# Unit 0's first two steps by chunks, seven products from unit 4, sums planned apart and a new order of work

## The chip, the cores and the metric

The kernel runs on one core of a Trainium2 chip. The metric is the device time of one execution in microseconds (us); of several runs the median is taken. An engine of the core runs its own queue of instructions in the order in which the program issued them, and waits on semaphores for the others: TensorE (PE, with its weight loads shown apart as PEld), VectorE (DVE), ScalarE (ACT), GpSimd (POOL) and SyncE (SP), which issues the transfers.

## The reference

A gated linear attention is followed by a layer pair. With B=4, H=8, S=768, D=48 and everything in fp32:

```python
for t in range(S):
    state = alpha[:, :, t, :, None] * state + np.einsum('bhd,bhe->bhde', k[:, :, t], v[:, :, t])
    y[:, :, t] = np.einsum('bhd,bhde->bhe', q[:, :, t], state)
# x: y as 3072 tokens x 384
h = x @ w_in               # 384 x 2048
g = h - np.tanh(h)
out = g @ w_out            # 2048 x 384
```

The two weight matrices arrive as float64 and are converted on the chip; the kernel computes in fp32.

## The kernel before, in words

The 3072 tokens are cut into 12 units of 256 tokens (three to a batch), and a unit into two chunks of 128. "u.c" names a chunk of a unit, "u:s" a step of a unit.

*Attention of a unit.* alpha, k and q (aT, kT, qT) are brought to columns by head and time. In units 0 and 1 TensorE does it with products by the identity ("turn aT", "turn kT", "turn qT", line 749) and a copy follows (line 753); later units load 32-row pieces, which ACT widens ("wide") and DVE transposes ("flip", line 717). DVE then runs scans over alpha: U (suffix products, line 796), "ends" (lines 804 and 805) and W (prefix products, line 815); k is multiplied by U ("kU") and q by W ("qW", line 761; in unit 0 each in halves a and b). "size" (line 824, ACT) squares U and W for a check of their range, "least" (DVE) does the same for the ends. TensorE makes "back" (k turned back for the update), copied out by ACT ("natural"), "scores" (line 884 in unit 0), which DVE masks ("masked", lines 908 and 911), "carried" (the product with the decayed state), the "update" of the state (line 1088), and "y". ACT copies y out as x ("x"), and DVE the part of it that is missing ("rest", line 1046 from unit 2 on); "moves" on SP brings rows together. From unit 2 on scores of a chunk and y of the chunk before are one visit of TensorE.

*The layers of a unit.* Eight steps of 256 hidden columns. "first" is the first product (line 1285 where plain: 12 matmuls of 128x256 per step); then ACT runs three passes over a 128x512 tile, "bend" (tanh, line 1326), "turn" (arctan, line 1329) and "square" (line 1334), and DVE multiplies by h ("shrunk", line 1338): that is g to the accuracy asked. "large" (line 1343, ACT, every second step) checks the range. "second" adds g @ w_out into four banks of PSUM, o0 to o3.

*Fewer products.* In units 0 and 1 "second" is plain (line 1361, four matmuls of 128x384 per step; unit 0 in o0 and o1, unit 1 in o2 and o3). From unit 2 on it is done with seven 128x192 products in place of eight (line 1383), for which DVE forms differences of g ("sums", lines 1350 and 1351) and, once, sums of w_out ("combine"). From unit SEVEN on (line 462, 3 before) "first" is done in such a way too: "first_a" (line 1298, four 128x128 products), a copy of one of them by ACT ("keep", line 1303), three dependent sums on DVE in one task ("partial", lines 1307 to 1309), "first" (lines 1314 and 1316) and a last sum on DVE ("join", line 1321). "weigh" prepares w_in for it once, "mix" x once per unit.

*The weights.* Sixteen pieces, in0 to in7 and out0 to out7, are fetched by SP into a pool of four buffers (line 45) and converted by two passes on ACT ("read_a", "read", lines 89 and 92) and two on DVE ("bits", line 96, and one that is named by the piece, such as "in0", line 99). A later part of the kernel loads them again to check their range ("reload", "look").

*The order.* Each of these is a task with an engine, a cost in microseconds, a rank and tasks that it follows. The order in which all tasks are issued is written out by hand as a list of steps (STEPS, line 335). Only inside the first stage does the planner add something: where its own sum of costs leaves TensorE idle before "y 0.0", it puts in small products of no use ("spin", line 1479, in bank o2). A tile of a pool with a fixed number of buffers (two banks "h" for first products, one pair "sc" for scores and y, o0 to o3) makes its next user wait for the last reader of the one before.

At the start the loads are issued as aT 0, v 0, kT 0, qT 0, in0, aT 1, in1, in2, in3, kT 1, qT 1, out0 and so on. Unit 0's steps use whole 256-token tiles, but for "first 0:0", which is made by chunks ("first_a 0:0" after "x 0.0", "first 0:0" after "x 0.1").

## Time and profile before

| | us |
|---|---|
| median of 3 runs (558.57 to 559.6) | 558.87 |
| profiled execution, whole | 563.36 |
| its span, first to last instruction | 561.6 |

| stretch of the profiled span (us) | length | PE busy | DVE busy | ACT busy | PE clock |
|---|---|---|---|---|---|
| 0 to 6.78 | 6.78 | 5.20 | 3.39 | 1.90 | 1.00 |
| 23.84 to 43.90 | 20.06 | 18.02 | 15.62 | 16.38 | 1.00 |
| 270.00 to 540.00 | 270.00 | 270.00 | 241.65 | 177.36 | 1.00 |

The stretches between these are in the prediction. In a row of groups of the profile stand the line of the kernel, the engine, the operation, "out<-in" by the program's tile names, the shape and the number of instructions; then busy time and mean length, and at the end the idle time of the engine before them with what released it. A wait written "PE h L1314 <- DVE w L1321: 1.7, 1, 1.7" says that TensorE, before the product of line 1314, waited 1.7 us in all, once, 1.7 at the longest, for DVE's instruction of line 1321. "issue" stands for idle time for which the profile shows no wait. A row of windows gives the stretch, its length, then busy time (and instructions) of PE, PEld, DVE, ACT and POOL, the granted clock of TensorE, the share of time in which the transfer engines were busy, and GB/s. In a timeline a row is the start, the time, engine, line and operation, and in brackets the idle time before it.

### The profile page before, as it was taken

The numbers are of one execution on the slowest core, as the hardware profiler recorded it, in microseconds if no ns is written. First come the engines' busy times: TensorE is split into PE (matmuls) and PEld (weight loads), VectorE is DVE, ScalarE is ACT, GpSimd is POOL, SyncE is SP. The second block draws the span as 40 slices with busy tenths as digits, with TensorE's granted clock in tenths as the row PEclk, the third lists the DMA queues.
The fourth block names the chain that finished last, engine by engine and source line by source line (L and its number), as shares of the span: only waits on it lengthen the run. The fifth ranks groups of instructions, "written<-read, shape, count | busy, mean of one in ns | idle before, by whom it ended". The sixth has DMA issues, their size and how long they took to land. (4 is left out here: it accounts for less than half of the span.)

```text
span 561.6 us, 15127 instructions
## 1 busy us (share of the span) xinstructions
PE 547.5 (97%) x6191; PEld 501.3 (89%) x6191; DVE 484.8 (86%) x1032; ACT 393.2 (70%) x746; POOL 4.9 (1%) x23
## 2 busy tenths in 40 slices
PE   7989999999999999998999999999999999999995
PEld 6877777777999999998999999999999999999995
DVE  7578659999989899999899999999999976796773
ACT  2589898967868768978668876757955654566460
POOL 3000000000000000000000000000000000000000
PEclk9699999999999999999999999999999999999999
DMA  9988482225264473535164251123020000100001
GB/s 219 240 202 245 169 204 84 88 65 146 52 135 101 114 128 107 115 117 140 35 121 113 85 157 50 48 48 85 15 51 1 30 2 8 36 2 1 30 2 33
DMA packets 60236, 50.90 MB, mean 91 GB/s; under 512 B 35552, under 2 KB 49920, under 8 KB 60160
## 3 DMA queue, kind: packets, MB, share of 16 engines
q1 hardware_dynamic: 57536, 49.07, 34.3%
q8 instruction: 51, 0.84, 0.6%
q10 hardware_dynamic: 2624, 0.79, 0.6%
q14 instruction: 25, 0.20, 0.1%
HBM read 44.04 MB, written 4.72 MB: 87 GB/s over the span
## 5 line engine op out<-in xcount | busy, mean ns | idle before, releaser
L1383 PE MATMUL o<-b,e 128*128 128x192 f32 x480 | 94.0, 326 | 0.0
L1326 ACT ACTIVATE z<-w 128x512 f32<-128x512 f32 x72 | 45.1, 626 | 54.8 <-DVE w L1321 54.7
L1383 PEld LDWEIGHTS o<-b,e 128*128 128x128 f32 x480 | 80.1, 190 | 0.8
L1383 PE MATMUL o<-w_out,e 128*128 128x192 f32 x320 | 78.6, 327 | 0.0
L1316 PE MATMUL h<-xT,w_in 128*128 128x256 f32 x288 | 74.1, 380 | 0.0
L1383 PE MATMUL o<-b,g 128*128 128x192 f32 x320 | 69.9, 326 | 0.0
L1285 PE MATMUL h<-xT,w_in 128*128 128x256 f32 (+1 forms) x300 | 66.2, 374 | 2.0 <-DVE g L1338 1.7
L1285 PEld LDWEIGHTS h<-xT,w_in 128*128 128x128 f32 x300 | 54.4, 190 | 10.9 <-DVE g L1338 1.8
L1329 ACT ACTIVATE z<-z 128x512 f32<-128x512 f32 x96 | 60.5, 630 | 1.8
L1334 ACT ACTIVATE u<-z 128x512 f32<-128x512 f32 x96 | 60.4, 629 | 1.9
L1321 DVE TENSOR_TENSOR w<-h,u 128x512 f32<-128x512 f32 x72 | 49.0, 681 | 11.8 <-PE h L1316 11.1
L1383 PEld LDWEIGHTS o<-w_out,e 128*128 128x128 f32 x320 | 55.7, 190 | 1.5
L1298 PE MATMUL h<-xT,w_in 128*128 128x128 f32 x288 | 56.4, 278 | 0.6 <-DVE w L1321 0.5
L1298 PE MATMUL h<-xT,w_out 128*128 128x128 f32 x288 | 55.8, 275 | 0.3 <-DVE xT L1245 0.3
L1383 PEld LDWEIGHTS o<-b,g 128*128 128x128 f32 x320 | 54.1, 190 | 0.4
L1316 PEld LDWEIGHTS h<-xT,w_in 128*128 128x128 f32 x288 | 49.2, 191 | 3.7
L1338 DVE TENSOR_TENSOR g<-w,u 128x512 f32<-128x512 f32 x72 | 48.8, 680 | 3.9 <-ACT u L1334 3.6
L1343 ACT ACTIVATE big<-u 128x1024 f32<-128x1024 f32 x48 | 50.7, 1055 | 0.9
L1298 PEld LDWEIGHTS h<-xT,w_in 128*128 128x128 f32 x288 | 46.7, 191 | 2.4 <-DVE w L1321 0.8
L1350 DVE TENSOR_TENSOR e<-g 128x384 f32<-128x384 f32 x80 | 43.8, 548 | 3.8 <-PE o L1383 3.3
L1303 ACT COPY u<-h 128x128 f32<-128x128 f32 x72 | 18.8, 262 | 38.2 <-PE h L1298 32.2
L1298 PEld LDWEIGHTS h<-xT,w_out 128*128 128x128 f32 x288 | 43.7, 192 | 0.5 <-DVE xT L1245 0.5
(177 smaller groups left out, 1134.9 us busy)
## 6 DMA issues: line engine op xcount, KB each, us to landing
raw<-in_moe_w_out_dram SPq DMA_DIRECT2D x16, 768.0 KB, 4.9
raw<-in_moe_w_in_dram SPq DMA_DIRECT2D x48, 96.0 KB, 4.4
raw<-in_moe_w_in_dram SPq DMA_DIRECT2D x16, 288.0 KB, 5.2
vt<-in_v_dram SPq DMA_DIRECT2D x23, 192.0 KB, 3.9
ar<-in_alpha_dram SPq DMA_DIRECT2D x20, 192.0 KB, 3.2
kr<-in_k_dram SPq DMA_DIRECT2D x20, 192.0 KB, 3.3
qr<-in_q_dram SPq DMA_DIRECT2D x20, 192.0 KB, 3.0
raw<-in_moe_w_in_dram SPq DMA_DIRECT2D x16, 192.0 KB, 4.3
```

What stands on the lines that cost most here:

```text
L1285: T.matmul(h[:, a, to], lhsT=w_in[:, j, f * P:(f + 1) * P], rhs=xT[u][:, j, to], start=(j == 0), stop=(j == KT - 1))
L1298: T.matmul(h[:, i], lhsT=left[n][:, s], rhs=right[u][n], start=i == 0, stop=True, skip_group_check=True)
L1303: A.copy(m["kept", s][:, 0], m["part", s][:, 0])
L1316: T.matmul(h[:, 2 * a:2 * a + 2].rearrange("p i t -> p (i t)"), lhsT=wi[:, KT - 1, s, a], rhs=xT[u][:, KT - 1, :], start=False, stop=True, ...
L1321: V.tensor_add(m["w", s], m["h", s].rearrange("p i t -> p (i t)"), m["u", s])
L1326: A.activation(m["z", s], m["h", s], AF.Tanh, scale=TA / W_SCALE)
L1329: A.activation(m["z", s], m["z", s], AF.Arctan, scale=TB)
L1334: A.activation(m["u", s], m["z", s], AF.Square, scale=TK * W_SCALE ** -0.5)
L1338: V.tensor_mul(g.rearrange("p a c t -> p (a c t)"), m["h", s], m["u", s])
L1343: A.activation(big, m["us", s // 2].rearrange("p s t -> p (s t)"), AF.Relu, bias=-F_FAST, scale=W_SCALE, accum_out=over[:, n:n + 1])
L1350: V.tensor_sub(e[:, 0:3, :], x[:, 3:4].to_broadcast([P, 3, P]), x[:, 0:3])
L1383: T.matmul(o[n][:, i], lhsT=g_, rhs=w_, start=(s_ == 0 and (n, i) in ((0, 0), (1, 0), (2, 1), (3, 0))), stop=(s_ == FS - 1), skip_group_ch ...
```

## The change

The attention of units 0 and 1 and the first steps are arranged anew, and the plain and the seven-product form change places in one unit:

- SEVEN goes from 3 to 4: unit 3's first products are plain, unit 3 has no "mix", "keep", "partial" and "join", and "weigh" moves one unit later.
- "rest" from unit 4 on is a copy on ACT, no longer on DVE.
- The three dependent sums of "partial" become three tasks, partial_a, partial_b and partial, which the order can place apart.
- Steps 0:0 and 0:1 (PARTED = 2) are made by chunks all the way: first, bend, turn, square, shrunk and second each stand once per chunk, with tiles of half the size ("first_a", "bend_a", ..., "second_0").
- Unit 0's output is in banks o2 and o1 and unit 1's in o0 and o3. The turns of unit 1, its "back" and its y use banks 0 and 3 in place of 2 and 3; "turn kT 1" follows "x 0.1" in place of "y 0.1".
- v 0 is loaded after kT 0 and qT 0, in0 after aT 1. The loads are now issued as qT 0, aT 0, kT 0, qT 1, aT 1, v 0, in0, in1, in2, kT 1, in3, v 1, out0 and so on.
- The planner's costs of some tasks are other numbers, and STEPS is a new list. On TensorE it opens with five spins, turn qT 0, turn aT 0, turn kT 0, five spins, back 0.0, a spin, update 0.0, scores 0.0, back 0.1, turn aT 1, scores 0.1, y 0.0, carried 0.1, update 0.1, y 0.1, turn qT 1, first_a 0:0, first 0:0, first_a 0:1, turn kT 1, first 0:1, back 1, first 0:2, first 0:3, scores 1.0, second_0 0:0, second 0:0, y 1.0.

```diff
...
     STEPS = (
...
     )
...
     PLAIN = 2
-    SEVEN = 3
+    PARTED = 2
+    SEVEN = 4
     BOTH_QUEUES = 0
...
-            add(f"fetch {what}{s}", "SP", 2.5 if both else 4.0 if what == "in" else 2.3, rank - 30, [held and f"read {held[0]}{held[1]}", held and f"bits {held[0]}{held[1]}"],
+            add(f"fetch {what}{s}", "SP", 2.5 if both else 4.0 if what == "in" else 2.3, rank - 30, [held and f"read {held[0]}{held[1]}", held and f"bits {held[0]}{held[1]}", n == 0 and "load aT 1"],
                 lambda what=what, s=s, both=both: fetch(what, s, False if both else None), lat=2.4)
...
             there = [f"fetch {what}{s}", both and f"upper {what}{s}", older and f"{older[0]}{older[1]}"]
-            add(f"read_a {what}{s}", "ACT", 1.05, rank, there, lambda do=do: do(0))
...
+            add(f"read_a {what}{s}", "ACT", 0.96, rank, there, lambda do=do: do(0))
...
 
...
                    [what < 3 and u > 0 and not by_matmul(u - 1, what) and not by_matmul(u, what) and f"{name}{prev}"]
-                   + [u == 1 and ("kUb 0" if what == 3 else "turn qT 0")]
+                   + [u == 1 and ("kUb 0" if what == 3 else "turn qT 0")] + [u == 0 and what == 3 and x for x in ("load kT 0", "load qT 0")]
                    + [f"{last} {u - 2}.{CU - 1}" if last != "y" or u - 2 < PLAIN else y_of((u - 2, CU - 1)) for last in ("y", "state") if what == 3 and u > 1
...
                     else:
-                        t = ps_o.tile([P, NP, P], FP32, name="turned", tag=f"o{2 * u + c}")
+                        t = ps_o.tile([P, NP, P], FP32, name="turned", tag=f"o{(0, 3)[c]}" if u else f"o{c}")
                     m["turned", what, c] = t.rearrange("p g (n i) -> p g i n", n=CU)
...
             if by_matmul(u, 1):
-                go("turn kT", "PE", 1.0, 1, ["load kT"] + [later and x for x in ("x 0.0", "y 0.1", "state 0.1")], lambda: turn(1))
+                go("turn kT", "PE", 1.0, 1, ["load kT"] + [later and x for x in ("x 0.0", "x 0.1", "state 0.1")], lambda: turn(1))
             if by_matmul(u, 2):
...
 
-                    m["y", c] = banks((2, 3))
+                    m["y", c] = banks((0, 3))
                     y = [m["y", c][b].rearrange("p g t -> p (g t)") for b in range(2)]
...
                         to = bass.AP(t.tensor, t.offset, [t.ap[0], (2 * TU + HP, 2), (1, HP)])
-                        V.tensor_copy(to, m["y", c].rearrange("p r g t -> p r (g t)")[0:ROWS, :, NP * (HP + D):])
+                        (A.copy if u >= 4 else V.tensor_copy)(to, m["y", c].rearrange("p r g t -> p r (g t)")[0:ROWS, :, NP * (HP + D):])
                         return
...
                     go_c("x", "ACT", 0.66, 10, [y, f"first {u - 2}:{FS - 1}"], features)
-                    go_c("rest", "DVE", 0.26, 10.5, [y, f"first {u - 2}:{FS - 1}"], rest)
+                    go_c("rest", "ACT" if u >= 4 else "DVE", 0.27, 10.5, [y, f"first {u - 2}:{FS - 1}"], rest)
                     return
...
             def back():
-                m["tp"] = banks((2, 3))
+                m["tp"] = banks((0, 3))
                 for c in range(CU):
...
 
+                parted = u == 0 and s < PARTED
+
+                def of_chunk(x, c):
+                    return x.rearrange("p (a t) -> p a t", a=2)[:, :, c * P:(c + 1) * P]
+
                 def first(to=slice(None)):
...
                                      start=(j == 0), stop=(j == KT - 1))
+                    m["h3", s] = h
                     m["h", s] = h if to.stop == P else h.rearrange("p a t -> p (a t)")
...
 
-                def partial():
+                def partial(n):
                     kept, part = m["kept", s], m["part", s]
-                    V.tensor_add(kept[:, 1], kept[:, 0], part[:, 1])
-                    V.tensor_add(kept[:, 2], kept[:, 1], part[:, 2])
-                    V.tensor_add(kept[:, 1::2], kept[:, 1:3], part[:, 3:4].to_broadcast([P, 2, P]))
+                    if n < 2:
+                        V.tensor_add(kept[:, n + 1], kept[:, n], part[:, n + 1])
+                    else:
+                        V.tensor_add(kept[:, 1::2], kept[:, 1:3], part[:, 3:4].to_broadcast([P, 2, P]))
 
...
 
-                def bend():
-                    m["z", s] = two.tile([P, 2 * TU], FP32, name="z")
-                    A.activation(m["z", s], m["h", s], AF.Tanh, scale=TA / W_SCALE)
+                def bend(c=None):
+                    if not c:
+                        m["z", s] = two.tile([P, 2 * TU], FP32, name="z")
+                    z, h = m["z", s], m["h", s]
+                    if c is not None:
+                        z, h = of_chunk(z, c), m["h3", s][:, :, c * P:(c + 1) * P]
+                    A.activation(z, h, AF.Tanh, scale=TA / W_SCALE)
+
+                def turn(c=None):
+                    z = m["z", s] if c is None else of_chunk(m["z", s], c)
+                    A.activation(z, z, AF.Arctan, scale=TB)
 
-                def turn():
-                    A.activation(m["z", s], m["z", s], AF.Arctan, scale=TB)
-
-                def square():
-                    if not seven:
+                def square(c=None):
+                    if not seven and not c:
                         take_u()
-                    A.activation(m["u", s], m["z", s], AF.Square, scale=TK * W_SCALE ** -0.5)
-
-                def shrunk():
-                    g = m["g", s] = three.tile([P, 2, CU, P], FP32, name="g")
+                    u_, z = m["u", s], m["z", s]
+                    if c is not None:
+                        u_, z = of_chunk(u_, c), of_chunk(z, c)
+                    A.activation(u_, z, AF.Square, scale=TK * W_SCALE ** -0.5)
+
+                def shrunk(c=None):
+                    if not c:
+                        m["g", s] = three.tile([P, 2, CU, P], FP32, name="g")
+                    g = m["g", s]
+                    if c is not None:
+                        h = m["h3", s][:, :, c * P:(c + 1) * P]
+                        V.tensor_mul(g[:, :, c, :], h, of_chunk(m["u", s], c))
+                        return
                     V.tensor_mul(g.rearrange("p a c t -> p (a c t)"), m["h", s], m["u", s])
...
                     if plain:
-                        if s == 0:
-                            m["o"] = [ps_o.tile([P, d_model], FP32, name=f"o{CU * u + c}") for c in range(CU)]
+                        if s == 0 and not of.start:
+                            m["o"] = [ps_o.tile([P, d_model], FP32, name=f"o{((2, 1), (0, 3))[u][c]}") for c in range(CU)]
                         for a in range(2):
                             f = 2 * s + a
-                            for c in range(CU):
+                            for c in range(CU)[of]:
                                 T.matmul(m["o"][c], lhsT=g[:, a, c, :],
...
                     plan.takes[f"first_a {me}"] = f"partial {me}"
-                plan.takes[f"first_a {me}" if u == s == 0 else f"first {me}"] = f"join {me}" if seven else f"shrunk {me}"
+                plan.takes[f"first_a {me}" if parted else f"first {me}"] = f"join {me}" if seven else f"shrunk {me}"
                 bank = None if older[2] else f"masked 0.{CU - 1}"
...
                     add(f"first_a {me}", "PE", 0.87, r, [bank, f"mix {u}", "weigh 1", late], seven_a)
-                    add(f"keep {me}", "ACT", 0.26, r + 0.1, [f"first_a {me}"] + old_u, keep)
-                    add(f"partial {me}", "DVE", 0.75, r + 0.2, [f"keep {me}"], partial)
+                    add(f"keep {me}", "ACT", 0.2, r + 0.1, [f"first_a {me}"] + old_u, keep)
+                    add(f"partial_a {me}", "DVE", 0.2, r + 0.2, [f"keep {me}"], lambda: partial(0))
+                    add(f"partial_b {me}", "DVE", 0.2, r + 0.21, [f"partial_a {me}"], lambda: partial(1))
+                    add(f"partial {me}", "DVE", 0.34, r + 0.22, [f"partial_b {me}"], lambda: partial(2))
                     add(f"first {me}", "PE", 1.51, r + 0.3, [f"first_a {me}", "weigh 2"], seven_b)
-                    add(f"join {me}", "DVE", 0.65, r + 0.7, [f"first {me}", f"partial {me}", older[2] and f"shrunk {older[2]}"], join)
-                elif u == s == 0:
+                    add(f"join {me}", "DVE", 0.61, r + 0.7, [f"first {me}", f"partial {me}", older[2] and f"shrunk {older[2]}"], join)
+                elif parted:
                     add(f"first_a {me}", "PE", 1.35, r, [f"in{s}", bank, "x 0.0"], lambda: first(slice(0, P)))
...
 
-                add(f"bend {me}", "ACT", 0.55, r + 0.9, [f"join {me}" if seven else f"first {me}", older[2] and f"square {older[2]}"], bend)
-                add(f"turn {me}", "ACT", 0.54, r + 0.92, [f"bend {me}"], turn)
-                add(f"square {me}", "ACT", 0.54, r + 0.95, [f"turn {me}"] + ([] if seven else old_u), square)
-                add(f"shrunk {me}", "DVE", 0.61, r + 1, [f"square {me}", older[3] and f"second {older[3]}"], shrunk)
+                if parted:
+                    for c, x in enumerate(("_a", "")):
+                        before = [f"{{}}_a {me}"] * c
+                        add(f"bend{x} {me}", "ACT", 0.32, r + 0.9, [f"first{x} {me}"] + [b.format("bend") for b in before], lambda c=c: bend(c))
+                        add(f"turn{x} {me}", "ACT", 0.32, r + 0.92, [f"bend{x} {me}"], lambda c=c: turn(c))
+                        add(f"square{x} {me}", "ACT", 0.32, r + 0.95, [f"turn{x} {me}"] + [b.format("square") for b in before], lambda c=c: square(c))
+                        add(f"shrunk{x} {me}", "DVE", 0.34, r + 1, [f"square{x} {me}"] + [b.format("shrunk") for b in before], lambda c=c: shrunk(c))
+                else:
+                    add(f"bend {me}", "ACT", 0.55, r + 0.9, [f"join {me}" if seven else f"first {me}", older[2] and f"square {older[2]}"], bend)
+                    add(f"turn {me}", "ACT", 0.54, r + 0.92, [f"bend {me}"], turn)
+                    add(f"square {me}", "ACT", 0.54, r + 0.95, [f"turn {me}"] + ([] if seven else old_u), square)
+                    add(f"shrunk {me}", "DVE", 0.61, r + 1, [f"square {me}", older[3] and f"second {older[3]}"], shrunk)
                 if s % 2:
...
                          + ([f"second {u}:{s - 1}"] if s else []))
+                if parted:
+                    older_a = [f"second_0 {u}:{s - 1}"] if s else []
+                    add(f"second_0 {me}", "PE", 1.29, r + 5, [f"out{s}", f"shrunk_a {me}"] + older_a, lambda: second(slice(0, 1)))
+                    add(f"second {me}", "PE", 1.29, r + 5.1, [f"shrunk {me}", f"second_0 {me}"] + needs, lambda: second(slice(1, 2)))
+                    return
                 parts = [7] if not seven or (u == NU - 1 and s >= FS - 2) else [2, 4, 5, 7]
```

## The prediction

> **What bounds the kernel now.** I read the page's totals and slices first, then the waits of TensorE alone, then windows cut where those waits lie, then the order of time on single engines.
>
> ```profile
> PE 547.5 (97%) x6191; PEld 501.3 (89%) x6191; DVE 484.8 (86%) x1032; ACT 393.2 (70%) x746; POOL 4.9 (1%) x23
> ...
> PEclk9699999999999999999999999999999999999999
> ```
> ```profile
> PE y L1088 <- issue: 1.9, 1, 1.9
> PE h L1314 <- DVE w L1321: 1.7, 1, 1.7
> PE h L1285 <- DVE g L1338: 1.7, 1, 1.7
> ```
> ```profile
> 6.78:13.60 6.82, 5.07 (x149) 4.07 (x147) 6.75 (x13) 2.03 (x5) 0.00 (x0) 1.00 1.13 248
> 13.60:23.84 10.24, 10.07 (x107) 8.38 (x111) 5.24 (x10) 4.92 (x10) 0.00 (x0) 0.50 0.91 216
> ...
> 27.20:43.90 16.70, 14.65 (x214) 12.89 (x213) 13.13 (x24) 14.23 (x23) 0.00 (x0) 1.00 0.84 211
> 43.90:204.00 160.10, 160.10 (x1758) 132.75 (x1757) 139.04 (x258) 131.46 (x233) 0.00 (x0) 1.00 0.50 127
> 204.00:270.00 66.00, 63.39 (x735) 59.99 (x735) 62.78 (x140) 53.59 (x108) 0.00 (x0) 1.00 0.46 116
> ```
> TensorE (PE) is the bound: from 43.9 to 204 it never rests. So time leaves only if the first 43.9 us shrink, if the rests at 204 to 270 (66.00 - 63.39 = 2.6) go, or if TensorE gets less work. VectorE (DVE) runs at 62.8 of 66 in that stretch: it causes those rests. In the opening TensorE rests for 1.92 us at 11.6 inside "update 0.0" for no wait that the profile shows, and from 13.60 to 23.84 its clock is 0.50.
>
> **The change, part by part.** The sum is made against the profiled execution (span 561.6, whole run 563.36) and then carried to the median of the plain runs, 558.87, which lies 4.5 us lower. Where those 4.5 us lie the profile can't say. If they are the rest at 11.6 and its half clock, what their removal brings is not there to be won from the median.
>
> *Seven products from unit 4, not 3.* Eight steps of unit 3 become plain.
>
> ```profile
> 82.26 5.34 PE L1285 MATMUL h<-xT,w_in 128*128 128x256 f32 x24
> 87.44 1.78 PE L1361 MATMUL o<-w_out,g 128*128 128x384 f32 x5
> ```
> Two plain steps take 87.44 - 82.26 = 5.18, one 2.59. A seven-product step is 0.89 ("first_a", 189.60 to 190.49) and 1.53 ("first", 200.58 to 202.11): 2.42. Eight steps cost TensorE 8 x 0.17 = +1.3 us, and all of it is on the path. DVE loses eight joins of 0.60, eight partial sums of 0.97 and one mix of 1.05 (start to start): 13.6 us.
>
> *"rest" to ScalarE (ACT) from unit 4.* 16 copies of 0.28 (line 1046, 279 ns): DVE 4.5 us less, ACT 4.5 more, in an engine at 53.6 of 66. It stands on ACT beside "x", which waited 11.3 us in all for TensorE, so I price it at nothing on the path; if each held up the next visit it would cost 4.5. DVE is rid of 18 us in all, mostly between 160 and 480. That should end the rests at 204 to 270: from -2.6 to +2 (a new order may put another wait there, and the largest there now is 1.7). I take -2.2.
>
> *The partial sums planned apart* add no instruction: three sums as before, now free to stand between other work. Priced inside the last item.
>
> *Opening.* q is loaded first, alpha second, v sixth. Now alpha's turn starts at 4.08 and takes 2.27; the copy starts at 6.43. In the new order the turn of q stands there, alpha's follows at 6.27 (partly at the faster rate of k's turn, 1.16) and the copy starts at 7.82: the scans begin 1.4 us later. The order of DVE from there:
>
> ```profile
> 6.43 0.69 DVE L753 COPY aT<-turned 128x512 f32<-128x512 f32 x1 [1.66 <-PE turned L749]
> 7.06 2.35 DVE L796 TENSOR_TENSOR_SCAN U<-aT,after 128x516 f32<-128x516 f32 x2
> 9.34 0.13 DVE L804 TENSOR_TENSOR ends<-U,low 128x4 f32<-128x4 f32 x1
> ...
> 16.69 1.29 DVE L908 TENSOR_TENSOR pm<-scores,mask 128x512 f32<-128x512 f32 x2 [2.10 <-PE scores L884]
> ...
> 20.17 1.29 DVE L908 TENSOR_TENSOR pm<-scores,mask 128x512 f32<-128x512 f32 x2 [1.46 <-PE scores L884]
> ```
> With start-to-start times: copy 0.63, two scans 2.30, both ends 0.54, kUa 0.58, Wa 1.16, kUb 0.58, qWa 0.58, Wb 1.15, least 0.1, qWb 0.6, decay 0.3: the first mask could start at 16.35 where it now waits until 16.69 for scores that run at half clock. If the clock stays whole, the scores are ready and DVE goes on: mask 1.25, bits 0.5, unit 1's copy 0.63 and a wait of 0.3 for its turn (whose bank qWb frees at 16.7), second mask 1.25: ends at 20.3 against 21.46. From there to the last kUb of unit 1: two scans 2.3, two bits 1.0, in0 to in2 2.75, ends, least, state and decay 1.1, two W scans 2.3, half a "shrunk" 0.35 (half of 0.68, an estimate), four products 2.4: 12.2, so 32.5. TensorE then does back 1 0.8, first 0:2 and 0:3 5.18, scores 1.0 1.07: its first second-layer product starts at 39.6. ACT has read w_out's first piece by then (37.3). Now that product starts at 43.92 with scores 1.0 undone, that is 45.0. Clean end of the range: -5.4.
>
> *The chunks* are why this closes: first 0:2 needs "shrunk 0:0", which now waits behind whole tiles on ACT until 36.5 (the 1.7 in the list, and a 0.37 behind it); with half tiles square 0:0 ends near 29.5. Twelve more instructions on ACT and two on DVE cost some 0.9 and 0.1 (a 128x512 tile takes 0.63, two halves an estimated 0.72), beside TensorE's work.
>
> *The other end.* If the rest in update 0.0 comes again with its half clock for 10.24 us, the masks end at 23.5, y 0.1 at 29.9, kUb at 38.4 and the product starts at 45.5: +0.5. Against it: the rests I find in the new order before 24 us are 0.3, 0.35 and 0.9 long, and the one that halved the clock was 2.1.
>
> *The value between.* DVE's two waits for scores in the rows above, 2.10 and 1.46, are what the half clock costs the kernel before: 3.6. If its plain runs are free of it, their product starts, scores 1.0 done, at 45.0 - 3.6 = 41.4, and a clean new opening wins only 1.8. The 4.5 us between the profiled and the plain time are about that size, so I take -2.2: near 1.8, with some weight on -5.4.
>
> The page TensorE: Matmul & The Clock Gate of the Trainium skill (Part 1) lets the clock fall after an idle window of about 3.4 us and rise after one busy window; here it fell after 2.1 us of rest and needed 10.24 us to rise. By the page the other end would be -2.9 rather than +0.5 (an estimate: 6.8 us less at half clock, half of it work); I keep the row. The page Runtime: NRT & Kernel Launch (Instruction fetch mechanics) calls the fetch of the next 16 KiB of instructions mostly hidden; a packet of the instruction queue lies just beside the 1.92 us rest, so by the trace it may not be.
>
> *Output banks* (unit 0 in o2 and o1, unit 1 in o0 and o3) move no work: each user still waits for the one before; the turn of k in unit 1 now waits for "x 0.1" too, which is done long before in the new order. Nothing, and 0.5 if x is late.
>
> *Unit 2's entry.* In the new order TensorE reaches "second 2:0" 2.5 us of work earlier, and DVE has 2.6 us more to do before its sums; the slack there now is 3.2 (store 1 ends at 138.2, the product starts at 141.4). 5.1 - 3.2 = 1.9 at worst; 0 if DVE starts the flips of unit 2 as much earlier as TensorE arrives. ACT's "wide" copies decide that; I take +0.6.
>
> Tail (last product 555.3, span 561.6): same work, same order, 0.
>
> Sum: +1.3 - 2.2 - 2.2 + 0.6 = -2.5, or 556.4.
>
> **Rivals.**
> 1. *All of it.* The plain runs of before have the half clock and the new ones don't, and no rest is left: -5.4 - 2.6 + 1.3 = -6.7, 552.2. For it: DVE gets 18 us of slack. Against it: 4.5 us of the profile's time are not in the plain runs.
> 2. *Hidden anyway.* DVE's flips of unit 2 start no earlier than now, at 80.5, because ACT carries 2 us more before them (sizeW 1 of 1.05 and the halves' 0.9) and is busy 33.5 of 36.1 from 43.9 to 80. Then what the opening wins is lost by second 2:0, and 1.9 with it: 1.9 + 1.3 - 2.2 = +1.0, 559.9. Against it: from 43.9 to 80 TensorE never waited for ACT.
> 3. *Slower: the rest and half clock stay, one place, update 0.0.* In the profiled form the opening costs +0.5 and the total is 559.2; if the plain runs of the kernel before are free of the half clock (3.6) and those of the new one are not, 562.8. It decides once the first second-layer product starts later than 46.4, since the other terms sum to -0.3. For it: no filler stands between back 0.1 and the turn of alpha, and alpha is later.
>
> **How the numbers follow.** Forecast 0.54 (its own range 554.2 to 558.4), rival 1 0.13, rival 2 0.17, rival 3 0.16. Plain runs of this kernel differ by about 0.2% (558.57 to 559.6), which is what can be told from no change. Faster by more (under 557.75): 0.13 and 0.48 of the forecast, 0.61. Within: the other 0.06 of it, 0.10 of rival 2 and 0.03 of rival 3, 0.19. Slower: 0.07 of rival 2 and 0.13 of rival 3, 0.20. The range reaches from rival 1 to above rival 2, and leaves out the far part of rivals 1 and 3: 552.0 to 560.8.
>
> **What would show it.** Right: clock 1.00 from about 7 us on; the copy of alpha near 7.8; the first 128x384 product near 40 to 43; DVE clearly under 60 in a 66 us stretch after 204, with no TensorE wait over 0.5 there; unit 3's steps at 2.59. Wrong: a rest of TensorE before 24 us with a clock of 0.50 after it; TensorE waiting for "e" or "w_out" between 44 and 140; a wait for the copies of "rest".

## The result, and the profile after

The changed kernel takes 560.38 us (median of 14 runs, 557.41 to 561.75), the kernel before, taken beside it, 559.05 (557.81 to 562.42). The ratio is 1.0009, with a 95% interval of 0.9989 to 1.0029: no difference that can be told. (The ratios here and below are estimated from the single runs; they are not the quotient of the two medians, which is 1.0024 here.) The prediction had 556.4 as likeliest and 552.0 to 560.8 as its range; the time lies inside the range, but the gain of 2.5 us that was forecast is not there, so the forecast was wrong.

Of 135 runs of the kernel before that the experiments took beside their kernels, 25 had a mean granted clock of 0.994 or less, with a median of 563.0, and the other 110 one of 0.996 or more, with a median of 559.7; the profiled execution that the prediction was worked out from (563.36, clock 0.989) is of the first kind.

The profiled execution of the changed kernel took 560.62 (span 558.9), near its median. Its totals and the row of granted clock in slices:

```profile
PE 545.6 (98%) x6151; PEld 497.5 (89%) x6151; DVE 466.4 (83%) x982; ACT 393.7 (70%) x760; POOL 4.9 (1%) x23
...
PEclk9999999999999999999999999999999999999998
```

The slice at 0.6 is gone, and VectorE has 18.4 us less to do (484.8 before). Then windows, cut like those of before (columns: stretch, length, busy time of PE, PEld, DVE, ACT and POOL, clock, share of transfers, GB/s):

```profile
13.60:23.84 10.24, 9.92 (x244) 8.09 (x243) 10.24 (x17) 8.51 (x17) 0.00 (x0) 1.00 0.93 229
43.90:204.00 160.10, 160.10 (x1647) 132.69 (x1636) 136.32 (x237) 133.44 (x235) 0.00 (x0) 1.00 0.51 131
204.00:270.00 66.00, 65.89 (x875) 62.75 (x873) 54.58 (x123) 49.35 (x105) 0.00 (x0) 1.00 0.39 95
270.00:300.00 30.00, 28.01 (x200) 26.59 (x193) 26.98 (x67) 23.44 (x51) 0.00 (x0) 1.00 0.55 132
```

The last of these stretches in the profile of before:

```profile
270.00:300.00 30.00, 30.00 (x323) 29.02 (x322) 28.13 (x66) 23.41 (x50) 0.00 (x0) 1.00 0.38 82
```

TensorE's rests between 204 and 270 went from 2.6 us to 0.11, as forecast. But 2.0 us of rest stand between 270 and 300, where there were none. From 13.6 to 23.84 it is VectorE that has no gap (10.24 of 10.24). TensorE's longest waits, and its order of time around the end of the opening:

```profile
PE h L1306 <- DVE u L1318: 1.6, 1, 1.6
...
PE h L1292 <- DVE w_in L99: 1.4, 1, 1.4
PE y L1164 <- DVE kT L763: 0.6, 1, 0.6
```
```profile
32.77 0.61 PE L1292 MATMUL h<-xT,w_in 128*128 128x256 f32 x2
34.73 5.02 PE L1292 MATMUL h<-xT,w_in 128*128 128x256 f32 x22 [1.35 <-DVE w_in L99]
...
40.74 2.85 PE L1384 MATMUL o<-w_out,g 128*128 128x384 f32 x8
```

The wait of 1.6 ends at 286.66, in front of a seven-product step; the product ahead of it starts at 284.7. The wait of 1.4 stands inside first 0:2, after its first matmul. The first second-layer product comes at 40.74; in the profile of before it is this row:

```profile
43.92 2.74 PE L1361 MATMUL o<-w_out,g 128*128 128x384 f32 x8
```

### The profile page after: what moved, and what is told of

The parts are those of the page before. It is cut to its first block, busy times and chain, and to the rows that moved or that the text cites. A ratio compares the mean times of both kernels' runs of the same rounds, so it can differ in the third digit from the quotient of the medians.

```text
span 558.9 us, 15009 instructions
## 1 busy us (share of the span) xinstructions
PE 545.6 (98%) x6151; PEld 497.5 (89%) x6151; DVE 466.4 (83%) x982; ACT 393.7 (70%) x760; POOL 4.9 (1%) x23
## 5 line engine op out<-in xcount | busy, mean ns | idle before, releaser
L1292 PE MATMUL h<-xT,w_in 128*128 128x256 f32 (+1 forms) x408 | 88.4, 369 | 1.4 <-DVE w_in L99 1.4
L1292 PEld LDWEIGHTS h<-xT,w_in 128*128 128x128 f32 x408 | 72.9, 190 | 12.5 <-DVE w_in L99 1.8
L1325 PE MATMUL h<-xT,w_in 128*128 128x256 f32 x256 | 65.9, 380 | 0.0
L1343 ACT ACTIVATE z<-z 128x512 f32<-128x512 f32 (+1 forms) x98 | 60.9, 621 | 1.9
L1351 ACT ACTIVATE u<-z 128x512 f32<-128x512 f32 (+1 forms) x98 | 60.7, 620 | 1.6
L1330 DVE TENSOR_TENSOR w<-h,u 128x512 f32<-128x512 f32 x64 | 43.9, 687 | 16.2 <-PE h L1325 15.2
L1306 PE MATMUL h<-xT,w_in 128*128 128x128 f32 x256 | 50.1, 277 | 1.7 <-DVE u L1318 1.6
L1306 PE MATMUL h<-xT,w_out 128*128 128x128 f32 x256 | 49.5, 275 | 0.5 <-issue 0.5
L1361 DVE TENSOR_TENSOR g<-w,u 128x512 f32<-128x512 f32 x64 | 43.6, 682 | 5.8 <-ACT u L1351 5.7
L1316 DVE TENSOR_TENSOR u<-u,h 128x128 f32<-128x128 f32 x128 | 34.6, 281 | 14.8 <-ACT u L1311 14.1
L1325 PEld LDWEIGHTS h<-xT,w_in 128*128 128x128 f32 x256 | 43.8, 191 | 3.3
L1373 DVE TENSOR_TENSOR e<-g 128x384 f32<-128x384 f32 x80 | 43.9, 549 | 3.2 <-PE o L1406 2.1
L1306 PEld LDWEIGHTS h<-xT,w_in 128*128 128x128 f32 x256 | 41.3, 191 | 3.2 <-issue 1.9
L1384 PE MATMUL o<-w_out,g 128*128 128x384 f32 x128 | 43.8, 488 | 0.0
```

Of the source, the lines that this page charges most:

```text
L1292: T.matmul(h[:, a, to], lhsT=w_in[:, j, f * P:(f + 1) * P], rhs=xT[u][:, j, to], start=(j == 0), stop=(j == KT - 1))
L1306: T.matmul(h[:, i], lhsT=left[n][:, s], rhs=right[u][n], start=i == 0, stop=True, skip_group_check=True)
L1325: T.matmul(h[:, 2 * a:2 * a + 2].rearrange("p i t -> p (i t)"), lhsT=wi[:, KT - 1, s, a], rhs=xT[u][:, KT - 1, :], start=False, stop=True, ...
L1330: V.tensor_add(m["w", s], m["h", s].rearrange("p i t -> p (i t)"), m["u", s])
L1343: A.activation(z, z, AF.Arctan, scale=TB)
L1351: A.activation(u_, z, AF.Square, scale=TK * W_SCALE ** -0.5)
```

## The experiments

A "rest" below is the time by which the distance of two TensorE records exceeds what is usual for their shape, over 0.15 us; its place is given by the start of the record ahead of it. It can be somewhat longer than a wait or a gap in the views, which count the modelled length of a record as busy. "Product" is the start of the first second-layer product. All kernels compute the whole reference.

**The kernel before once more (k0).** No edit.

> The kernel before, unchanged, to have a second profile of it and a measure of how far two equal kernels differ. Theory A: the profile of before that the prediction was worked out from (563.36) is not its usual run; in the usual one TensorE does not rest in update 0.0 and its clock stays 1.00 from 13.6 to 23.8 us, so a new profile has a span near 557 and its first 128x384 product near 40. Theory B: the half clock belongs to the kernel, and the new profile shows it again, with the product near 44. Ratio 1.000 within 0.002.

Measured: 560.42 (557.85 to 565.99; before, beside it, 560.16), ratio 1.0027, 0.9997 to 1.0058. The second profile (557.85, span 556.1), a window and TensorE's order of time:

```profile
13.60:23.84 10.24, 10.24 (x191) 8.72 (x192) 9.31 (x16) 8.90 (x16) 0.00 (x0) 1.00 1.00 212
```
```profile
11.34 0.31 PE L1088 MATMUL y<-vt,kn 128*64 128x48 f32 x3
12.95 0.55 PE L1088 MATMUL y<-vt,kn 128*48 128x48 f32 x13 [1.30 <-issue]
...
38.57 2.74 PE L1361 MATMUL o<-w_out,g 128*128 128x384 f32 x8
```

Theory A holds on what matters: the rest in update 0.0 stays (1.30, against the theory), but the clock stays whole, and the product comes at 38.57, which is 5.3 earlier than in the first profile. With scores 1.0 (1.07) still to do that is 39.64, and the changed kernel's 40.74 is 1.1 later. The profile is near the fast end of its runs (median 560.42).

**The two halves apart (k1, k2).** The changed kernel's opening with the old form and order behind it, and the reverse:

```diff
 k1, from the changed kernel:
-    SEVEN = 4
+    SEVEN = 3
 rest on VectorE; order: the new one up to "first 2:0", then the old one
 k2, from the kernel before:
-    SEVEN = 3
+    SEVEN = 4
 rest on ScalarE from unit 4, sums apart; order: the old one up to "first 2:0", then the new one
```

> The changed kernel's opening (loads, chunks, output banks, its order up to the first step of unit 2) with the kernel before's form and order behind it (seven products from unit 3, rest on DVE, sums together). Theory A (the plain runs of before have no half clock, so the opening wins only what the chunks and the order win beside it): 0 to -2 us, 557 to 559. Theory B (the opening wins 4.25 us as the two profiles show, and the rest of the change loses as much): -4 us, 555.

> The other half: the kernel before's opening up to the first step of unit 2, then the changed kernel's form and order (seven products from unit 4, rest on ACT, sums apart). Theory A: unit 3 costs 1.3 and the rests of 204 to 270 only move to 270 to 300: +0.5 to +2 us, near 560. Theory B: +4 us or more, 563, to undo the opening's 4.25.

Measured: k1 564.43 (before 560.16; ratio 1.0066, 1.0033 to 1.0099), k2 563.31 (1.0054, 1.0026 to 1.0082). Both are slower than either whole kernel. Theory B's -4 for the opening is refused, and Theory A's ranges (0 to -2 and +0.5 to +2) were missed too; that k2 has Theory B's 563 says little, since it was to undo a gain that k1 doesn't have. The two halves don't add up to the whole: the seam makes waits of its own. The waits of TensorE in k1 show two that neither kernel has:

```profile
PE h L1296 <- DVE g L1365: 1.5, 1, 1.5
...
PE h L1327 <- ACT xT L1071: 0.9, 1, 0.9
```

They lie at 130.3 and 195.6, behind the seam; k2 has one of 1.0 at 141.1. The profiled executions (562.72 and 560.18) lie 1.7 and 3.1 under the medians, so the profiles don't show all that the halves lose; that stays open. What the two do show is the openings, which lie ahead of the seam: product at 40.30 in k1, and at 39.13 + 1.07 = 40.20 in k2, 0.1 apart.

**Rest back on VectorE, and rest alone on ScalarE (k3, k7).**

```diff
 k3, from the changed kernel:
-    go_c("rest", "ACT" if u >= 4 else "DVE", ...)
+    go_c("rest", "DVE", ...)
 k7, from the kernel before:
-    go_c("rest", "DVE", ...)
+    go_c("rest", "ACT" if u >= 4 else "DVE", ...)
```

> The changed kernel with the copies of rest back on VectorE. Theory A (rest on ScalarE costs nothing, since x beside it ends later): 0 to +1 against the changed kernel, for VectorE has 4.5 us more to do. Rival C (rest on ScalarE holds up the moves and with them the mix of a unit): the wait of 2.6 us for the moved rows before the mix of unit 6 shrinks, -1 to -2 against the changed kernel.

> The kernel before with one part of the change alone: the copies of rest on ScalarE from unit 4 on, in the same order. Theory D (VectorE bounds 204 to 270, and rest 4.1 there stands 2 us behind x 4.1 and so holds the moves of unit 4): the rest of 0.6 at 208.9 goes and that of 1.9 at 263 shrinks, -0.6 to -1.5 us. Rival: ScalarE holds the copies up as VectorE did, 0 to +1.

Measured: k3 561.46 (ratio 1.0020, 0.9989 to 1.0051), not to be told from the changed kernel, as Theory A had it. In its profile the rest near 287 is 2.4 long and not shorter, so rival C falls. Its window between 204 and 270:

```profile
204.00:270.00 66.00, 65.51 (x757) 62.43 (x756) 54.05 (x121) 48.99 (x102) 0.00 (x0) 1.00 0.39 93
```

So with rest on VectorE too the changed kernel has almost no rest there (0.49): the other parts of the change are enough for that. In the order of before it is different. k7 557.12 where the kernel before had 560.01: ratio 0.9945, 0.9921 to 0.9969. That is one sixteen-copy part of the change, and it is faster than both kernels. Its rests after the product sum to 1.7, where k0 has 4.7. Its window, and under it the same of k0:

```profile
204.00:270.00 66.00, 65.14 (x660) 62.05 (x661) 64.05 (x140) 53.87 (x110) 0.00 (x0) 1.00 0.42 111
```
```profile
204.00:270.00 66.00, 63.24 (x640) 60.04 (x639) 62.93 (x138) 52.49 (x106) 0.00 (x0) 1.00 0.45 111
```

TensorE's rest there is 0.86 and not 2.76. The rest of 1.9 at 259 and the one of 0.6 behind it are gone; the one before the first mix of unit 4 (0.9 at 204) is not, so Theory D is right on the rest of 1.9 and wrong on the one before the first mix, which it had at 208.9. Whether what counts is VectorE's load or the earlier moves, as the theory has it, was not tried apart.

**The changed kernel once more (k4).** No edit.

> The changed kernel, unchanged, beside the others of this call: a second profile of it. Theory A (in their usual runs both kernels have a whole clock, and then the new opening is slower): its first 128x384 product stands again near 40.7, about 1.1 later than in the second profile of the kernel before (38.57, and scores 1.0 of 1.07 still to do), and the ratio is 1.001 to 1.005. Theory B: product under 39.6, ratio under 0.998.

Measured: 561.19 (before 560.01; ratio 1.0010, 0.9987 to 1.0033). The order of time of TensorE:

```profile
41.20 2.85 PE L1384 MATMUL o<-w_out,g 128*128 128x384 f32 x8
```

Theory A again. Over the profiles with a whole clock, the old opening has its product, with the 1.07, at 39.64 to 40.20 (six: k0, k2, k6, k7, k8, k10) and the new one at 40.30 to 41.22 (four: the one after, k1, k4, k5): about 0.9 later.

The same profiles show where these 0.9 come from. "Whole from" is where the trace's record of the granted clock begins, at 1.00; "scans" is the start of VectorE's first scan over alpha; the product of the old opening has the 1.07 added.

| opening | profile | whole from | scans | product | scans to product |
|---|---|---|---|---|---|
| old | k0 | 5.74 | 6.87 | 39.64 | 32.77 |
| old | k2 | 5.97 | 6.91 | 40.20 | 33.29 |
| old | k6 | 5.64 | 6.79 | 39.95 | 33.16 |
| old | k7 | 5.88 | 6.95 | 40.17 | 33.22 |
| old | k8 | 6.97 | 7.10 | 39.91 | 32.81 |
| old | k10 | 6.95 | 7.08 | 39.92 | 32.84 |
| new | k1 | 5.05 | 7.63 | 40.30 | 32.67 |
| new | after | 6.13 | 8.06 | 40.74 | 32.68 |
| new | k4 | 7.18 | 8.53 | 41.20 | 32.67 |
| new | k5 | 7.09 | 8.55 | 41.22 | 32.67 |

From the scans on, the new opening takes the same 32.67 to 32.68 four times, on average 0.3 less than the old one; but its scans start 1.24 later. And its scans depend on when TensorE's clock becomes whole, those of the old one hardly: of the 64x64 products of the first turns, those ahead of that moment come 27 to 33 ns apart and those behind it 14 to 17, so the first ones run at half speed, although the windows print 1.00 for a stretch without a record (that of 0 to 6.78 in the table of before is such a one). In the new order alpha's turn waits behind q's slow one.

**What stands behind the rest at 284.7 (k5).** In the changed kernel the DMA queue of SP and, in a second view, VectorE's order of time there:

```profile
271.65 1.79 SPq L45 DMA_DIRECT2D raw<-in_moe_w_in_dram  x4
273.54 1.01 SPq L623 DMA_DIRECT2D vt<-in_v_dram  x2
274.66 7.60 SPq L1187 DMA_DIRECT2D xT<-xT  x6
```
```profile
283.57 0.29 DVE L1246 TENSOR_TENSOR xT<-xT 128x128 f32<-128x128 f32 x1 [2.58 <-DMA xT<-xT]
```

x and rest of unit 6 end at 272.4. The moves that follow them (xT to xT) start 2.3 later, behind four pieces of a weight that is loaded once more to be checked, and one of their six issues takes 3.3 (all six 7.6). VectorE stands 2.58 us in front of the mix of unit 6 until they land, with the sums of unit 5 queued behind, which first_a waits for. The edit, in the order of SP:

```diff
 load qT 8
-reload 11
 load v 8
 moves 6
+reload 11
 (reload 12 to 15 and their looks on ScalarE one slot later)
```

> The changed kernel with the order of one place altered: on SP the moves of unit 6 stand ahead of the eleventh check load of the weights, and that load and the later ones, with their passes on ScalarE, come one slot later. Theory M (the rest of 1.8 us at 284.7 comes from moves that wait on SP behind a load of the weights' check, then the mix, then the sums of VectorE): the rest goes, -1.8 us, and with it a half clock that it can start. Rival (the rest is VectorE's own load, at 27 of 30 us there): it stays at 1.5 or more.

Measured: 559.04 (before 560.01, the changed kernel beside it 561.19): ratio 0.9978, 0.9960 to 0.9996. Its window:

```profile
270.00:300.00 30.00, 29.80 (x303) 28.67 (x295) 28.93 (x70) 23.50 (x51) 0.00 (x0) 1.00 0.47 110
```

The rest is gone (0.2 left of 30), and 2.1 us with it. The six issues now take 3.8 in all, the longest 0.65. Theory M holds.

**The same in the kernel before with rest on ScalarE (k10).** Reload 5 goes behind moves 4, and later ones one slot on.

> The kernel before with rest on ScalarE, and on SP the moves of unit 4 ahead of the check load of the weights that stood before them (that load and the later ones one slot later). Theory M: TensorE's rest of 0.9 at 204 before the first seven-product step of unit 4 goes, and 0.2 behind it: -0.8 to -1.1 against the version with rest alone. Rival: VectorE is late there anyway: 0.

Measured: 558.13 (before 559.75), ratio 0.9968, 0.9947 to 0.9989, which is not better than k7's 0.9945, where Theory M had -0.8 to -1.1. The rest at 204 went (TensorE is busy for 65.94 of the 66 us), but rests of 0.6, 0.4 and 0.5 stand at 311, 354 and 356, where k7 has 0.3 in all, and one of 0.7 without a wait at 53. The mechanism was right; the later rests give what it brought back, though 3 of the 12 runs of k10 and none of the 9 of k7 also have a mean clock under 0.995. What makes the later rests was not followed up.

**Where the rest in update 0.0 comes from (k6).** The kernel before; two runs of three fillers of 128 columns become one filler of 384 each:

```diff
-spin, spin, spin            # 128 columns each
+spin(after[:, 0:3 * P])     # 384 columns
```

> The kernel before with four TensorE instructions fewer ahead of update 0.0: two fillers of 384 columns in place of two runs of three of 128, the same work. Theory F (the rest of 1.3 to 1.9 us in update 0.0 is the fetch of instructions, at a fixed place in TensorE's stream): the rest moves four matmuls later, from after the third record of update 0.0 to after about the eleventh, and keeps its length. Rival G (it belongs to what update 0.0 reads): it stays after the third record. Time within 0.2% of the kernel before under both.

Measured: 559.71, ratio 0.9991 (0.9971 to 1.0011). Its order of time of TensorE, to be held against that of k0 above:

```profile
11.26 0.55 PE L1088 MATMUL y<-vt,kn 128*64 128x48 f32 x11
13.48 0.33 PE L1088 MATMUL y<-vt,kn 128*48 128x48 f32 x5 [1.67 <-issue]
```

Three records before the rest have become eleven: four matmuls fewer ahead, four matmuls (of two records each) later. The rest belongs to a place in TensorE's stream of instructions and not to what update 0.0 reads. Theory F holds on the place. That it is the fetch is argued from this and from a packet of 16 KB of the instruction queue that lies there (in k0 from 10.09 to 11.49, the rest from 11.65 to 12.95; in k6 from 10.81 to 12.20, the rest from 11.81 to 13.48), and not shown.

**Unit 3 alone (k8).** From k7:

```diff
-    SEVEN = 3
+    SEVEN = 4
 order: as in k7, weigh 3 behind first 3:3 and weigh 4 behind first 3:7
```

> The kernel before with rest on ScalarE (the run before this one, 557.12 where the kernel before had 560.01) and one part of the change more: seven products from unit 4 on, in the same order but for what the missing tasks force. Theory U (a plain step costs TensorE 0.17 more, and the rests around the first mix move with it): +1.3 to +2.5 against the version with rest alone. Rival (VectorE's 13.6 us less work in unit 3 is worth more): 0 to -1.

Measured: 561.84 (before 559.75), ratio 1.0033 (1.0006 to 1.0060): 4.7 above k7's median, more than either said. TensorE's work after the product grows by 1.8 (509.68 against 507.87). Its rests after the product grow by 2.2, of which 1.5 come at 180.4, where VectorE waits 3.0 for first 3:3 before weigh 3, which this order put there. So Theory U's sign is right. Work and rests make up the 3.4 between the two profiles (560.32 and 556.88), less 0.3 at the product and 0.3 in the tail; the medians lie 1.3 further apart than the profiles, and what makes that is not shown.

**What the wait inside first 0:2 is for (k9).** In the changed kernel:

```diff
-in3
 first 0:2
+in3
```

> The changed kernel with one task moved in the order: the last pass of the conversion of in3 is issued behind first 0:2 in place of ahead of it. Theory W (first 0:2, which reads only in2, waits for in3 since the two regions of w_in interleave, and the order of issue decides which waits): the rest of 1.5 us after the first matmul of first 0:2 goes, in3 then starts when first 0:2 has ended, and first 0:3 waits 0.9 for it: -0.4 to -0.6 at the first second-layer product (41.2 to 40.7). Rival (first 0:2 waits for in2 or for its half tiles): no change.

Measured: 561.39 (before 559.75), ratio 1.0025 (1.0002 to 1.0048). TensorE, then VectorE:

```profile
32.82 2.77 PE L1295 MATMUL h<-xT,w_in 128*128 128x256 f32 x12
37.96 2.83 PE L1295 MATMUL h<-xT,w_in 128*128 128x256 f32 x12 [2.37 <-DVE g L1362]
```
```profile
35.72 0.96 DVE L99 CUSTOM_DVE_ANT_0 w_in<-bits,more 128x1536 uint16<-128x1536 uint16 x1 [2.59 <-PE h L1295]
```

First 0:2, which reads only the columns of in2, now runs without a wait. Instead VectorE holds in3 back for 2.59 until first 0:2 has ended, although it writes other columns. So the two are put in order of issue, and Theory W's mechanism is right. That it is by regions that interleave fits the place of the wait: w_in is one tile of three blocks, a piece writes its columns in each of them, and in the profile after the wait falls behind the matmul of the first block. Its time was wrong: behind in3 on VectorE stands the second half of shrunk 0:1, which frees the bank of first 0:3, so the wait is 2.37 and not 0.9, and the product comes later: at 41.78, which is 33.67 after the scans where the unchanged opening has 32.67.

**The same used in the kernel before (k11).** From k10:

```diff
+in2
 first 0:1
-in2
+square 0:0
 bend 0:1
-square 0:0
```

> As the run above, and in the opening two tasks moved: the last pass of in2 is issued ahead of first 0:1 and square 0:0 ahead of bend 0:1. Theory W: VectorE no longer waits 2.2 us for first 0:1 before it writes in2, and TensorE's rest of 1.7 us before first 0:2 goes: -1.0 to -1.7 against the run above. Rival (ScalarE's reading of w_in decides): 0 to -0.4.

Measured: 557.10 (554.56 to 558.23; before 559.75), ratio 0.9944, 0.9922 to 0.9966. TensorE's order of time, and VectorE's pass of in2 (k0 had it at 28.32, after 2.20 of wait for TensorE):

```profile
30.79 2.86 PE L1287 MATMUL h<-xT,w_in 128*128 128x256 f32 x12
...
37.48 2.74 PE L1363 MATMUL o<-w_out,g 128*128 128x384 f32 x8
```
```profile
25.40 0.96 DVE L99 CUSTOM_DVE_ANT_0 w_in<-bits,more 128x1536 uint16<-128x1536 uint16 x1 [0.62 <-ACT more L92]
```

First 0:2 starts without a rest, and the product comes 1.37 earlier than in k10 (38.85). Two moved tasks do to the old opening what the chunks were to do. This version and k7 are faster than both kernels.

**Which part makes the new opening late (l1, l2, l3).** In the changed kernel alpha is loaded and turned ahead of q again:

```diff
+load aT 0
 load qT 0
-load aT 0
+turn aT 0
 turn qT 0
-turn aT 0
```

> The changed kernel with one part of the change undone: alpha is loaded and turned first and q second, as in the kernel before. Theory S (q first makes the scans start 1.0 later, 8.06 against 7.06, and that is what the new opening loses): the copy of alpha starts near 6.4 and the first second-layer product comes 0.8 to 1.0 earlier than 41.2. Theory T (ScalarE, full from 13.6 to 26, and the wait for in3 set the end of the opening): scans earlier, product earlier by 0.3 at most.

> As the run above, with the moves of unit 6 ahead of the check load too. The two do not touch: the gain of the moves (559.04 where the changed kernel had 561.19) and what the run above gives add up; 1.8 to 2.8 us under the changed kernel, about 0.997 of the kernel before or less.

Measured: l1 561.94 (before 559.65), ratio 1.0031 (1.0003 to 1.0060); l2 559.63, ratio 0.9994 (0.9969 to 1.0019). In l1's expectation ScalarE is named as full where the row of the changed kernel's profile has VectorE without a gap (10.24 of 10.24) and ScalarE at 8.51. The copy of alpha starts at 6.00, yet the product comes at 43.40. The order of time of TensorE in l1 tells why:

```profile
10.80 3.61 PE L1520 MATMUL spin<-after,ident 128*128 128x512 f32 x8
...
15.16 1.16 PE L889 MATMUL scores<-qT,kT 48*128 48x128 f32 x16
```

The planner's own costs now show it a longer gap ahead of update 0.0, and it fills it with four wide products of no use; scores 0.0 starts 0.75 later than in k4 (14.41), though its q was there at 12.6. A fall of the clock adds to it (below); l2, with the same opening and a whole clock, has its product at 42.15, which is 34.98 after the scans. So l1's time told nothing on its question, and l2, which adds the moves of unit 6, gave the gain of the moves (2.3 against l1) and not the 1.8 to 2.8 against the changed kernel that were expected. In l3 three of the four are left out:

```diff
+if wide > 3: continue      # no fourth and later filler of 512 columns
```

> The changed kernel with alpha loaded and turned first, as in the run before this one, but without three of the four wide fillers that the planner then put ahead of update 0.0 (3.6 us of products of no use, behind which scores 0.0 started at 15.16 though its q was there at 12.6). Theory S: scores 0.0 starts near 13, 1.4 earlier than in the changed kernel, and the first second-layer product comes 0.8 to 1.0 earlier than 41.2. Theory T (ScalarE and the wait for in3 set the end): earlier by 0.3 at most. Either may be undone where TensorE now rests long enough for its clock to fall, or waits for instructions again.

```profile
13.66 1.16 PE L889 MATMUL scores<-qT,kT 48*128 48x128 f32 x16
...
40.46 2.85 PE L1387 MATMUL o<-w_out,g 128*128 128x384 f32 x8
```

Measured: 560.04 (before 559.74), ratio 0.9999 (0.9976 to 1.0022). Its scans start 1.07 earlier than in k4 (7.46 against 8.53) and its product 0.74 earlier than 41.20: nearer to Theory S than to T. One product at 40.46 alone would not show it, since unchanged openings have 40.30 to 41.22. Taken in pairs with nearly the same start of the whole clock, the scans do:

| whole from | q first: scans | alpha first: scans |
|---|---|---|
| 5.05 and 5.37 | 7.63 (k1) | 6.80 (l1) |
| 6.13 and 6.19 | 8.06 (after) | 7.17 (l2) |
| 7.78 and 7.87 | 8.88 (k3) | 7.46 (l3) |

To load and turn q first costs the scans 0.8 to 1.4, and from them on the unchanged opening takes a fixed time; so this order is what makes it late. With the scans of the old one (6.95 on average) its product would be at 39.6 to 40.0 (an estimate, with 32.67 and with l3's 33.00), no later than the old one's 40.0. The wait for in3 inside first 0:2, in l3 1.50, is untouched by it.

## Why the prediction was wrong, point by point

An account from the product on makes the terms comparable. From it to TensorE's last product, without the rests, the second profile of before has 507.81 us of work and 4.74 of rests, the first 507.78 and 3.59, the profile after 508.04 and 3.44.

- *The base of the sum, and the opening (-2.2).* This is the step that failed: the opening does not win 2.2 us, it loses about 0.9. "The value between" took -2.2, "with some weight on -5.4", for a kernel before that has the half clock in part of its runs. Against the first profile the new opening wins 43.92 + 1.07 - 40.74 = 4.25, near the clean end of 5.4. Against runs with a whole clock it loses about 0.9 (1.1 against k0). I had doubted the base and put the old opening without the half clock at 41.4; it is 39.64 to 40.20, on average 40.0, since its two waits for scores (3.6) were not all that the half clock cost: VectorE's next wait for TensorE, 2.17 at 24.57 in the first profile, is gone in k0 but for 0.69 in two waits. That is 1.4 of the miss. The other 1.3 is the new opening, which I put at 39.6 and which takes 40.9 on average.
- *q first.* "The scans begin 1.4 us later" was near (8.06 against 6.87 in k0, 1.24 on average). I took the delay to be covered by waits for scores; in a whole clock there is 0.24 of such wait ahead of the first mask, VectorE then has no gap, and it goes through to the product, which follows the scans by 32.67 each time.
- *The chunks.* Square 0:0 ends at 30.2 where I had 29.5, and shrunk 0:0 no longer holds first 0:2. But the 1.7 us became a wait of 1.35 for in3 and one of 0.6 for kUb 1. I had looked only for what first 0:2 reads; k9 and k11 show that in3 and in2 bind it by their place in the order.
- *Seven from unit 4 (+1.3).* Right: work after the product is 508.04 - 507.81 + 1.07 = +1.3 (the same account gives 1.5 for k2 and 1.8 for k8, so it is good to some 0.5).
- *The rests at 204 to 270 (-2.2).* They went, as I had it, by more than one of the parts: k3 lacks them with rest on VectorE, and k7, in the order of before and with rest on ScalarE alone, loses 1.9 of the 2.76. There that copy is worth 0.55%, and not nothing on the path as I priced it; in the changed kernel (k3) it is worth nothing that can be told. In the changed kernel 2.0 us came back at 270 to 300, because the moves of unit 6 wait on SP behind a check load (k5). The bound "a new order may put another wait there" had it; the value that I took did not. I had followed VectorE's order and not SP's. From the first profile to the one after, rests after the product fall by 0.15 in all.
- *Unit 2's entry (+0.6).* Nothing: TensorE is busy for the whole 160.10 us from 43.9 to 204.
- *The sums apart and the output banks.* No wait names them; neither was tried alone.
- *The tail (0).* From TensorE's last product to the span's end lie 5.0 us in k0, 6.3 in the first profile and 6.7 after, for the same work. Over the 17 profiles it is 5.0 to 6.9, so it changes from one execution to the next by more than what I called nothing.

Together, against k0: +1.1 + 1.3 - 1.3 (rests) + 1.7 (tail) = +2.8, which is the difference of the spans (558.9 and 556.1). k0 is near the fast end of its kernel, so the medians lie only 1.3 apart. Rival 2 has the time (559.9) without its mechanism. Rival 1 fell with the base, and rival 3 asked for a half clock in the new runs; 2 of 26 had a mean clock under 0.995. (Rival 3's 559.2 should be 559.1: 558.87 - 0.3 + 0.5.)

Every sign that I had named for being right came: a whole clock from about 7 us, the copy of alpha at 7.26, the product at 40.74, VectorE at 54.58 of 66 and no wait over 0.5 in that stretch, two steps of unit 3 in 5.18. None of those for being wrong came. They are all signs in the new kernel alone, and the step that failed was about the old one's usual run and about the difference of the two.

## What to carry to other kernels

Ask first whether the profiled execution is a usual run: 4.5 us between its time and the median, and a slice of clock at 0.6, were as large as all that was to be judged, and a sum made against such a profile books a gain that the median does not have. When one engine is freed of work, follow the queue that feeds the next stage as well: here the rest came back because six small moves stood behind a load that nobody waited for. A part that is "beside other work" (sixteen copies of 0.28 us) can be the best of a change in an order where others wait for the engine it leaves (k7), and worth nothing in another (k3); try the parts alone before joining them.

## What the runs showed of the hardware

*Rests without a wait.* TensorE rests 0.8 to 1.9 us at one place of its stream in the old opening, in all profiles that have it, and the place moves with the number of instructions ahead of it (k6). In the changed kernel's profiles the packet lies elsewhere (from 8.67 to 9.63 in the profile after, under wide fillers that start at 8.64), and no rest without a wait is seen ahead of the product. The page Runtime: NRT & Kernel Launch of the Trainium skill (Instruction fetch mechanics) calls the cost of crossing a 16 KiB block of instructions mostly hidden; if the rest is that fetch, it costs 0.8 to 1.9 us here.

*The clock falls by chance and for different times.* In k3 the same two rests that the changed kernel has (0.6 and 1.34) were followed by half a clock. Windows of k3, in which the clock is the number ahead of the last two:

```profile
31.00:35.00 4.00, 2.56 (x19) 1.76 (x17) 3.36 (x7) 3.10 (x7) 0.00 (x0) 1.00 1.02 280
35.00:39.00 4.00, 3.45 (x9) 2.86 (x10) 1.72 (x4) 3.97 (x9) 0.00 (x0) 0.57 1.03 302
```

0.57 over 4 us is 3.4 us at half speed, and l1 shows the same between 36 and 40. In the trace's own record each fall ahead of TensorE's last product lasts 3.41 (two in k3, one in k9, one in l1) or, in the first profile of before, three times that, 10.24. The page TensorE: Matmul & The Clock Gate (Part 1) has the clock rise after one busy window of about 3.4 us: k3 and l1 agree with it, the first profile (TensorE busy for 10.07 of the 10.24) does not, and I had weighed the rule by that one profile alone. Rests of 1.3 to 2.1 us in all were followed by a fall in some profiles and not in others of the same opening (1.92 in the first profile, but not 1.67 in k6 or 1.80 in k2; 0.6 and 1.34 in k3, but not the same in k4 and k5), so what a rest of this size costs is a chance and not a fixed price.
